# Part of the softmax exps moved from ScalarE to VectorE in a two-layer transformer kernel

## The chip, the cores and the metric

The kernel runs on one core of one Trainium2 chip. The metric is the time of one execution on the device in microseconds (us), lower is better. An execution is called slow when it is over 1.5% above the fastest of the same kernel; only fast ones are compared. A ratio within 2% of 1 counts as "the same".

A word on terms. A **block** is 128 keys by 512 queries of one head. A **slot** is one step of the main loop: three blocks, thus one exp instruction over 1536 columns. A **segment** is four heads with 512 queries against all 2048 keys: 64 blocks, 21.3 slots. A **chunk** is 512 queries of one layer, all 32 heads: eight segments. **Side work** is everything TensorE does beside attention: projections, output, feed-forward, transposes. A piece of it is **evacuated** when VectorE copies its sum out of PSUM. To **emit** an instruction is to put it into an engine's queue while the kernel is being built; the order is fixed then.

## The reference, cut to what matters

Two layers; in each, attention with 32 heads of 16 on 2048 rows of width 512, then a relu feed-forward of width 1792. Inputs are bf16.

```python
scores = jnp.einsum("bhqd,bhkd->bhqk", q, k) * (Dh ** -0.5)
p = _softmax(scores, axis=-1)
o = jnp.einsum("bhqk,bhkd->bhqd", p, v)
...
x = x + _A_ref(_layernorm(x, axis=-1), A_wqkv, A_wo)     # attention
x = x + _B_ref(_layernorm(x, axis=-1), B_w1, B_w2)       # feed-forward
# both twice, with the same weights
```

The softmax takes 2 x 32 x 2048 x 2048 exps. With 128 lanes that is 2.1 million columns, in 4096 blocks of 512.

## The kernel before: the parts that matter

The main loop. Each slot writes scores for three blocks into one of two PSUM tiles of three banks, one exp reads them all, and the value matmuls of the slot before last follow. Side work is given to TensorE in small pieces by a pace, and VectorE's own queue by a budget.

```python
    while blocks:
        ...
        now = [blocks.popleft() for _ in range(min(W, len(blocks)))]      # W = 3
        b = ps_s[no % 2]                                                   # two tiles, three banks each
        times = 1 if level >= 0 else 2 if level > -1 else 3                # repeats, to keep TensorE busy
        for _ in range(times):
            for w, (sg, kb, g) in enumerate(now):
                nc.tensor.matmul(b[:, w, :], kt[...], qbuf[...], start=True, stop=True, ...)
        ex = nc.scalar.activation(out=eb[:, :m, :], in_=b[:, :m, :], func=ACTF.Exp, scale=SCALE)
        run_evac()
        while len(pend) > 1:
            emit_pv()                                                      # value matmuls into ps_o
        spent = run_pe(pace) if todo else 0.0                              # side work, a little a slot
        level = min(level + times + 1 + spent - FLOOR, 0.4)
        run_dve(900)
```

The function that is used when something must be finished before the loop may go on. Its order: first evacuations, then every piece of TensorE work whose inputs have been emitted, and VectorE's queue last.

```python
    def force():
        if evac:
            run_evac()
            return True
        if cur or pick(emitted):
            cur.popleft()[1]()
            return True
        for i, (c, deps, fn) in enumerate(dve_q):
            if emitted(deps):
                dve_q.pop(i)
                fn()
                return True
        return False

    def run_until(key):
        while key not in made:
            assert force(), key
```

All side work shares one PSUM bank, `ps_f`, during the main loop.

The softmax here doesn't subtract the row's maximum and nothing guards it: scores larger than these inputs give would overflow.

## Time and profile before

| | before |
|---|---|
| median of 4 runs | 2046.97 us (2044.28 to 2048.04) |
| span of the profiled run | 2037.9 us |
| busy: ScalarE, TensorE, VectorE | 92%, 83%, 21% |
| score matmuls (4096 are needed) | 7704 |
| ScalarE idle ahead of exps | 55.1 us |
| mean TensorE clock | 0.971 |

The lines are shown and read in the prediction. One more view of the same trace is the table of waits: who waited for whom, then us in total, times, and the longest.

```profile
PE ps_s L621 <- ACT e L628: 218.8, 604, 0.8
...
ACT e L628 <- PE ps_s L621: 54.2, 109, 2.4
```

The two lines together say which engine leads. TensorE waits for ScalarE four times as long as ScalarE for TensorE, and ScalarE's longest wait is 2.4 us.

### The profile page before, as it was taken

To read this page: it belongs to the slowest core of one execution; us is meant where nothing else is said; L and a number is where in the kernel's file an instruction comes from. 1 tells how busy PE (TensorE), PEld (TensorE's weight loads), DVE (VectorE), ACT (ScalarE), POOL (GpSimd) and SP (SyncE) were. 2 spreads that over 40 slices of the span, in tenths; PEclk is the share of its full clock that TensorE was granted. 3 is DMA by queue.
4 is the path that set the end of the run, shared out by engine and by line. 5 is a ranking of instruction groups with operands and counts; after the bars stand their busy time and mean duration, and the time that the engine had idled before them with its cause. 6 is when DMAs were issued, how large, how long until landed. Compare 5 with 4: busy or idle time off the path is not lost.

```text
span 2037.9 us, 30025 instructions
## 1 busy us (share of the span) xinstructions
PE 1690.9 (83%) x13604; PEld 523.4 (26%) x13604; DVE 436.9 (21%) x927; ACT 1871.7 (92%) x1407; POOL 2.4 (0%) x35
## 2 busy tenths in 40 slices
PE   5777778888888888888889877898888888888876
PEld 2222222222222222222222222222222222222222
DVE  5111102212132132212133220211112111121122
ACT  2799999999999999999989999999999999999960
POOL 0000000000000000000000000000000000000000
PEclk8999999999999999999899989989998999989998
DMA  4000000000000000000000010000000000000000
GB/s 155 1 12 12 12 7 12 12 12 6 12 12 11 7 12 12 10 8 12 12 1 1 4 30 9 9 12 12 17 12 12 10 12 19 12 9 10 17 11 11
DMA packets 34131, 29.42 MB, mean 14 GB/s; under 512 B 17492, under 2 KB 25428, under 8 KB 34004
## 3 DMA queue, kind: packets, MB, share of 16 engines
q1 hardware_dynamic: 32420, 25.94, 5.6%
q8 instruction: 106, 1.74, 0.3%
q10 hardware_dynamic: 1584, 1.57, 0.2%
q14 instruction: 21, 0.17, 0.0%
HBM read 7.86 MB, written 2.10 MB: 5 GB/s over the span
## 4 chain that ended last, share of the span: by engine, by line
ACT 71%; PE 17%; DVE 8%; DMA 3%; issue 1%; SPq 0%; DVEq 0%
ACT e L628 71%; PE ps_s L621 6%; PE ps_f L243 5%; PE ps_o L545 4%; DMA r<-u 2%; PE ps_s L243 2%; DVE u L494 1%; DVE ht L400 1%; DVE q L371 1%; PE ps_s L579 1%; DVE stats L260 1%; DMA u<-c 1%; PE ps_f L298 0%; DVE xn L288 0%; ACT xnT L573 0%
## 5 line engine op out<-in xcount | busy, mean ns | idle before, releaser
L628 ACT ACTIVATE e<-ps_s 128x1536 bf16<-128x1536 f32 x1366 | 1847.9, 1581 | 55.1 <-PE ps_s L621 54.2
L621 PE MATMUL ps_s<-q,ktp 32*128 32x512 bf16 x7704 | 812.2, 385 | 221.2 <-ACT e L628 218.8
L545 PE MATMUL ps_o<-e,vaug 128*32 128x512 bf16 x4096 | 568.7, 396 | 45.3 <-DVE u L494 34.6
L621 PEld LDWEIGHTS <-ktp 32*128 32x128 bf16 x7704 | 257.2, 92 | 714.5 <-issue 659.7
L545 PEld LDWEIGHTS <-vaug 128*32 128x32 bf16 x4096 | 138.1, 93 | 490.3 <-issue 490.3
L243 PE MATMUL ps_f<-xn2T,w 128*128 128x512 bf16 x400 | 121.2, 391 | 11.1 <-DVE q L371 5.1
L400 DVE TENSOR_SCALAR ht<-ps_f 128x512 bf16<-128x512 f32 x99 | 68.4, 691 | 281.0 <-PE ps_f L243 281.0
L243 PE MATMUL ps_f<-w,ht 128*128 128x512 bf16 x406 | 120.0, 383 | 1.0
L499 DVE SCALAR_TENSOR_TENSOR ot<-u,mask,r 128x512 bf16<-128x512 f32 (+1 forms) x67 | 48.7, 727 | 276.5 <-DMA r<-u 273.8
L494 DVE COPY u<-ps_o 128x512 f32<-128x512 f32 x58 | 40.1, 691 | 266.5 <-PE ps_o L545 266.5
L243 PE MATMUL ps_f<-xnT,wqkv 128*128 128x512 bf16 x248 | 74.1, 389 | 1.4 <-DVE vaug L363 0.2
L371 DVE TENSOR_SCALAR q<-ps_f,mask 128x512 bf16<-128x512 f32 x68 | 47.9, 746 | 90.2 <-PE ps_f L243 90.2
L243 PE MATMUL ps_f<-wo,ot 128*128 128x512 bf16 x224 | 66.2, 386 | 0.8
L414 DVE TENSOR_TENSOR x<-x,ps_f 128x512 bf16<-128x512 bf16 x29 | 20.0, 688 | 189.2 <-PE ps_f L243 189.2
L386 DVE TENSOR_TENSOR x<-x,ps_f 128x512 bf16<-128x512 bf16 x28 | 19.2, 687 | 161.1 <-PE ps_f L243 161.1
L243 PEld LDWEIGHTS <-w 128*128 128x128 bf16 x448 | 32.0, 99 | 76.4 <-issue 67.5
L260 DVE BATCH_NORM_STATS2 stats<-x 128x6 f32<-128x512 bf16 x64 | 44.0, 687 | 7.0 <-DMA x<-in_A_x_dram 5.6
L338 DVE CAST ktp<-ps_f 128x512 bf16<-128x512 f32 x28 | 19.4, 692 | 117.1 <-PE ps_f L243 117.1
L243 PEld LDWEIGHTS <-ht 128*128 128x128 bf16 x448 | 29.1, 97 | 57.5 <-issue 47.9
L398 ACT ACTIVATE ht<-ps_s 128x512 bf16<-128x512 f32 x6 | 3.6, 597 | 42.8 <-PE ps_s L243 42.8
L298 PE MATMUL ps_f<-ident,xn 128*128 128x128 bf16 x188 | 21.8, 249 | 16.3 <-DVE xn L288 10.0
L298 PEld LDWEIGHTS <-xn 128*128 128x128 bf16 x256 | 18.4, 109 | 54.6 <-DVE xn L288 31.7
(54 smaller groups left out, 303.1 us busy)
## 6 DMA issues: line engine op xcount, KB each, us to landing
r<-u SPq DMA_DIRECT2D x63, 256.0 KB
w<-in_B_w_dram SPq DMA_DIRECT2D x2, 1792.0 KB
x<-in_A_x_dram SPq DMA_DIRECT2D x16, 128.0 KB
out_dram<-x SPq DMA_DIRECT2D x16, 128.0 KB
wqkv<-in_A_wqkv_dram ACTq DMA_DIRECT2D x3, 512.0 KB
c<-u SPq DMA_DIRECT2D x63, 8.0 KB
u<-c SPq DMA_DIRECT2D x63, 8.0 KB
wo<-in_A_wo_dram SPq DMA_DIRECT2D x1, 512.0 KB
```

Of the source, the lines that this page charges most:

```text
L243: nc.tensor.matmul(b, lhsT, rhs, start=(i == 0), stop=(i == n - 1))
L260: nc.vector.bn_stats(out=st[:], in_=x_t[j * TPC + i][:])
L298: nc.tensor.transpose(pt[:, c * P : (c + 1) * P], xnbuf[i][:, c * P : (c + 1) * P], ident[:])
L371: nc.vector.tensor_scalar(out=qbuf[n % 2][e][:], in0=b, scalar1=mask[e][:, 0:1], scalar2=None, op0=ALU.mult,)
L400: nc.vector.tensor_scalar(out=ht[ft][:], in0=b, scalar1=0.0, scalar2=None, op0=ALU.max)
L414: nc.vector.tensor_add(out=x_t[tt][:], in0=x_t[tt][:], in1=b)
L494: nc.vector.tensor_copy(out=u[:], in_=ps_o[:])
L499: nc.vector.scalar_tensor_tensor(out=ot[t][:, a : a + w], in0=u[:, a : a + w], scalar=mask[e][:, 0:1], in1=r[:, a : a + w], op0=ALU.mult, ...
L545: nc.tensor.matmul(ps_o[32 * g : 32 * g + 32, :], vaug[sg["l"]][kb][:, 4 * sg["T"] + g, 2 * e : 2 * e + 32], s["e"][:, w, :], start=(kb == ...
L579: nc.tensor.matmul(b, lhsT, rhs, start=(i == 0), stop=(i == len(mms) - 1))
L621: nc.tensor.matmul(b[:, w, :], kt[32 * g : 32 * g + 32, kc : kc + P], qbuf[sg["n"] % 2][sg["e"]][32 * g : 32 * g + 32, :], start=True, sto ...
L628: ex = nc.scalar.activation(out=eb[:, :m, :], in_=b[:, :m, :], func=ACTF.Exp, scale=SCALE)
```

## The change

Its intent: ScalarE is the bound and VectorE idles, so in six of a segment's 21 slots the third block's exp is made by VectorE. The queries are scaled so that a score is already in units of 2 to the 23rd per octave; adding 126 x 2^23 and converting to an integer gives the bits of a float whose exponent is right and whose mantissa is linear. Two bit operations and a polynomial in the mantissa give the rest. Of the two parts of the result one is doubled, and the addition is left to the value matmul: three matmuls a block in place of one. The blocks of two slots (a **pair**) share the five long VectorE operations. Because the VectorE values come out divided by 2 x LEAD, the exps on ScalarE get a bias of -ln(2 x LEAD), from a [128,1] tile. Which pairs are taken, and when their operations are emitted, is decided by a counter `load[0]` of VectorE's backlog. The core of the diff (cuts marked):

```diff
+    PAIRS = ((0, 2), (6, 8), (12, 14))
     FLOOR = 3.4
+    BACKLOG = 5000.0
...
-        while i < len(dve_q) and budget > 0:
+        while i < len(dve_q) and load[0] < limit:
...
+    def flush_pair():
+        run_until(pairs[0]["key"])
+        emit_pair()
+
+    def dve_block(half, sg, kb, g, src):
+        while half == 0 and pairs:
+            flush_pair()
+        nc.vector.tensor_scalar(
+            out=di[:, half, :].bitcast(I32), in0=src, scalar1=EXP_BIAS, scalar2=0.0,
+            op0=ALU.add, op1=ALU.max,
+        )
+        load[0] += 690
...
+            dve_q[0:0] = [
+                (650, [], lambda: bits(dm, 0x007FFFFF, 0x3E800000)),
+                (1220, [], lambda: step(dy, dm, C2, dm)),
+                (1220, [], lambda: step(dy, dy, C1, dm)),
+                (1220, [], lambda: step(de, dy, C0, di)),
+                (650, [], last),
+            ]
+
+    def emit_pair():
+        p = pairs.popleft()
...
+        for rhs in (de, de, None):
+            for half, (kb, g) in halves:
+                pv(p["sg"], kb, g, tops[:, half, 1::2] if rhs is None else rhs[:, half, :])
...
+            if half == 0:
+                taken = load[0] + sum(c for c, _, _ in dve_q) < BACKLOG
...
-        ex = nc.scalar.activation(out=eb[:, :m, :], in_=b[:, :m, :], func=ACTF.Exp, scale=SCALE)
+        ex = nc.scalar.activation(
+            out=eb[:, :m, :], in_=b[:, :m, :], func=ACTF.Exp, bias=ebias[:, 0:1],
+            scale=1.0 / (LOG2E * UNIT),
+        )
...
+        load[0] = max(load[0] - 50.0 - 427.0 * m, 0.0)
         run_evac()
+        if half is not None:
+            dve_block(half, sg, kb, g, b[:, W - 1, :])
...
+        if pairs and ready([pairs[0]["key"]]):
+            emit_pair()
...
-        run_dve(900)
+        run_dve(500.0)
```

It also adds, where a segment is finished, `run_until(("m", n - 2))`: the multiply that normalises the segment before last must have been emitted.

More of the change, by code (lines that the diff above doesn't have):

```diff
@@ L1 @@
+import math
 from contextlib import ExitStack
@@ L55 @@
     NACC = 6
+    LEAD, C2, C1, C0 = 0.43216083424908747, -0.036015386827967774, 0.769178243088122, 0.36146642138144963
+    KAPPA_BITS = 0x00170000
+    LOG2E = 1.4426950408889634
+    UNIT = float(1 << 23)
+    EXP_BIAS = 126.0 * UNIT
+    PAIRS = ((0, 2), (6, 8), (12, 14))
     FLOOR = 3.4
+    BACKLOG = 5000.0
     ctx.enter_context(tc.manual_schedule())
@@ L66 @@
     mask = [sb([P, 1], FP32, f"mask{e}") for e in range(2)]
+    qmask = [sb([P, 1], FP32, f"qmask{e}") for e in range(2)]
+    ebias = sb([P, 1], FP32, "ebias")
     wqkv = sb([P, NDC, 3 * D], BF16, "wqkv")
@@ L89 @@
     ot = [sb([P, QS], BF16, f"ot{t}") for t in range(NT)]
-    acc = [sb([P, QS], FP32, f"acc{t}") for t in range(NACC)]
+    dm = sb([P, 2, QS], FP32, "dm")
+    dy = sb([P, 2, QS], FP32, "dy")
+    di = sb([P, 2, QS], FP32, "di")
+    de = sb([P, 2, QS], BF16, "de")
+    acc = [x[:, k, :] for x in (dm, dy, di) for k in range(2)]
     ebuf = [sb([P, W, QS], BF16, f"e{n}") for n in range(NE)]
@@ L121 @@
     nc.gpsimd.memset(warm[:], 0.0)
+    nc.gpsimd.memset(ebias[:], -math.log(2.0 * LEAD))
     nc.scalar.activation(out=warm[:], in_=warm[:], func=ACTF.Exp)
@@ L189, in run_pe, with run_dve @@
         return spent
-    def run_dve(budget):
+    load = [0.0]
+    def run_dve(limit):
         i = 0
-        while i < len(dve_q) and budget > 0:
+        while i < len(dve_q) and load[0] < limit:
             c, deps, fn = dve_q[i]
@@ L197, in run_dve @@
                 fn()
-                budget -= c
+                load[0] += c
             else:
@@ L203, in run_evac @@
         while evac:
-            evac.popleft()()
+            c, fn = evac.popleft()
+            fn()
+            load[0] += c
     def force():
@@ L228, in run_all, with mm_group @@
         assert not (urgent or work or dve_q or cur)
-    def mm_group(mms, fin, deps, per=2):
+    def mm_group(mms, fin, deps, per=2, cost=690):
         hold = {}
@@ L244, in piece @@
                 if a + per >= n:
-                    evac.append(lambda: fin(b))
+                    evac.append((cost, lambda: fin(b)))
             pieces.append((min(per, n - a), piece))
@@ L324, in fin @@
                     mark(("xnT", tag, i))
-                evac.append(fin)
+                evac.append((430, fin))
             groups.append({"pieces": [(1.3, piece)], "deps": [("xn", tag, i)] + war})
@@ L371, in fin @@
                 nc.vector.tensor_scalar(
-                    out=qbuf[n % 2][e][:], in0=b, scalar1=mask[e][:, 0:1], scalar2=None,
+                    out=qbuf[n % 2][e][:], in0=b, scalar1=qmask[e][:, 0:1], scalar2=None,
                     op0=ALU.mult,
@@ L378, in q_group @@
             [(wqkv[:, c, T * P : (T + 1) * P], xnT[j][:, c, :]) for c in range(NDC)],
-            fin, all4("xnT", ("ln1", l, j)),
+            fin, all4("xnT", ("ln1", l, j)), cost=1400,
         )
@@ L460, in add_run @@
                     "l": l, "j": j, "t": 2 * T + e, "e": e, "T": T, "kbs": kbs, "n": n,
-                    "load": load, "store": store,
+                    "load": load, "store": store, "begun": set(),
                 }
@@ L483, in finish_segment @@
         l, j, t, e = sg["l"], sg["j"], sg["t"], sg["e"]
+        load[0] += 690
         if sg["store"]:
-            nc.vector.tensor_copy(out=acc[t][:], in_=ps_o[:])
+            nc.vector.tensor_copy(out=acc[t], in_=ps_o[:])
             return
@@ L488, in finish_segment @@
         norm_no[0] += 1
+        if n > 1:
+            run_until(("m", n - 2))
         u, r, c = ubuf[n % 2], rbuf[n % 2], cbuf[n % 2]
@@ L491, in finish_segment @@
         if sg["load"]:
-            nc.vector.tensor_add(out=u[:], in0=acc[t][:], in1=ps_o[:])
+            nc.vector.tensor_add(out=u[:], in0=acc[t], in1=ps_o[:])
         else:
@@ L504, in mul @@
                 mark(("ot", l, j, t, i))
+            mark(("m", n))
         if last:
@@ L533, with pv @@
     pend = deque()
-    last_exp = [None] * NE
+    exps = [deque(maxlen=6) for _ in range(NE)]
+    def pv(sg, kb, g, rhs, stop=False):
+        e = sg["e"]
+        nc.tensor.matmul(
+            ps_o[32 * g : 32 * g + 32, :],
+            vaug[sg["l"]][kb][:, 4 * sg["T"] + g, 2 * e : 2 * e + 32],
+            rhs, start=g not in sg["begun"], stop=stop,
+            tile_position=(0, 32 * g), skip_group_check=True,
+        )
+        sg["begun"].add(g)
     def emit_pv():
@@ L543, in emit_pv @@
             sg, kb, g, w = s["blocks"].popleft()
-            e = sg["e"]
-            nc.tensor.matmul(
-                ps_o[32 * g : 32 * g + 32, :],
-                vaug[sg["l"]][kb][:, 4 * sg["T"] + g, 2 * e : 2 * e + 32],
-                s["e"][:, w, :],
-                start=(kb == sg["kbs"][0]), stop=(kb == sg["kbs"][-1]),
-                tile_position=(0, 32 * g), skip_group_check=True,
-            )
-            if kb == sg["kbs"][-1] and g == 3:
+            last = kb == sg["kbs"][-1]
+            if last:
+                while pairs and pairs[0]["sg"] is sg:
+                    flush_pair()
+            pv(sg, kb, g, s["e"][:, w, :], last)
+            if last and g == 3:
                 finish_segment(sg, sg is segs[-1])
@@ L555, in emit_pv, with bits, step, last @@
             pend.popleft()
+    pairs = deque()
+    pair_no = [0]
+    def flush_pair():
[3 more added lines that the diff above has]
+        while half == 0 and pairs:
+            flush_pair()
+        nc.vector.tensor_scalar(
+            out=di[:, half, :].bitcast(I32), in0=src, scalar1=EXP_BIAS, scalar2=0.0,
+            op0=ALU.add, op1=ALU.max,
+        )
+        load[0] += 690
+        if half == 0:
+            pair_no[0] += 1
+            pairs.append({"sg": sg, "key": ("e", pair_no[0]), "blocks": []})
+        pairs[-1]["blocks"].append((kb, g))
+        if half == 1:
+            key = pairs[-1]["key"]
+            def bits(out, keep, put):
+                nc.vector.tensor_scalar(
+                    out=out[:].bitcast(I32), in0=di[:].bitcast(I32), scalar1=keep,
+                    scalar2=put, op0=ALU.bitwise_and, op1=ALU.bitwise_or,
+                )
+            def step(out, x, c, y):
+                nc.vector.scalar_tensor_tensor(
+                    out=out[:], in0=x[:], scalar=c, in1=y[:], op0=ALU.add, op1=ALU.mult
+                )
+            def last():
+                bits(di, 0x7F800000, KAPPA_BITS)
+                mark(key)
+            dve_q[0:0] = [
[7 more added lines that the diff above has]
+        p = pairs.popleft()
+        halves = list(enumerate(p["blocks"]))
+        tops = di[:].bitcast(BF16)
+        for rhs in (de, de, None):
+            for half, (kb, g) in halves:
+                pv(p["sg"], kb, g, tops[:, half, 1::2] if rhs is None else rhs[:, half, :])
     for j in range(NQS):
@@ L568 @@
                     op=ALU.add, axis=mybir.AxisListType.XY,
+                )
+            for e in range(2):
+                nc.vector.tensor_scalar(
+                    out=qmask[e][:], in0=mask[e][:], scalar1=SCALE * LOG2E * UNIT, scalar2=None,
+                    op0=ALU.mult,
                 )
@@ L599 @@
     level = 0.0
+    taken = False
     while blocks:
@@ L626 @@
                 )
-        m = len(now)
-        ex = nc.scalar.activation(out=eb[:, :m, :], in_=b[:, :m, :], func=ACTF.Exp, scale=SCALE)
-        if last_exp[no % NE] is not None:
+        sg, kb, g = now[-1]
+        r = (kb * 4 + g - 2) // W
+        half = None
+        if len(now) == W and now[0][0] is sg and not (sg["load"] or sg["store"]):
+            half = next((p.index(r) for p in PAIRS if r in p), None)
+            if half == 0:
+                taken = load[0] + sum(c for c, _, _ in dve_q) < BACKLOG
+            if not taken:
+                half = None
+        m = len(now) - (half is not None)
+        ex = nc.scalar.activation(
+            out=eb[:, :m, :], in_=b[:, :m, :], func=ACTF.Exp, bias=ebias[:, 0:1],
+            scale=1.0 / (LOG2E * UNIT),
+        )
+        for earlier in exps[no % NE]:
             tc.declare_no_dep(
-                ex.ins, last_exp[no % NE],
+                ex.ins, earlier,
                 reason="the matmuls that read the buffer between the two writes order them",
             )
-        last_exp[no % NE] = ex.ins
+        exps[no % NE].append(ex.ins)
+        load[0] = max(load[0] - 50.0 - 427.0 * m, 0.0)
         run_evac()
+        if half is not None:
+            dve_block(half, sg, kb, g, b[:, W - 1, :])
         for sg, kb, g in now:
@@ L639 @@
             emit_pv()
-        pend.append({"e": eb, "blocks": deque(x + (w,) for w, x in enumerate(now))})
+        if pairs and ready([pairs[0]["key"]]):
+            emit_pair()
+        pend.append({"e": eb, "blocks": deque(x + (w,) for w, x in enumerate(now[:m]))})
         rest = len(blocks) / W % per_chunk
@@ L644 @@
         spent = run_pe(pace) if todo else 0.0
+        sg = now[-1][0]
         level = min(level + times + 1 + spent - FLOOR, 0.4)
-        run_dve(900)
+        run_dve(500.0)
     while pend:
```

## The prediction

> **What bounds the kernel now.** I read, in this order, the busy shares, the costliest groups, the chain in order of time, the timeline of a stretch in mid-run, and the busy time of one tile by windows. Busy shares and groups of the page:
>
> ```profile
> PE 1690.9 (83%) x13604; PEld 523.4 (26%) x13604; DVE 436.9 (21%) x927; ACT 1871.7 (92%) x1407; POOL 2.4 (0%) x35
> ...
> L628 ACT ACTIVATE e<-ps_s 128x1536 bf16<-128x1536 f32 x1366 | 1847.9, 1581 | 55.1 <-PE ps_s L621 54.2
> L621 PE MATMUL ps_s<-q,ktp 32*128 32x512 bf16 x7704 | 812.2, 385 | 221.2 <-ACT e L628 218.8
> ...
> L545 PE MATMUL ps_o<-e,vaug 128*32 128x512 bf16 x4096 | 568.7, 396 | 45.3 <-DVE u L494 34.6
> ...
> L400 DVE TENSOR_SCALAR ht<-ps_f 128x512 bf16<-128x512 f32 x99 | 68.4, 691 | 281.0 <-PE ps_f L243 281.0
> ...
> L499 DVE SCALAR_TENSOR_TENSOR ot<-u,mask,r 128x512 bf16<-128x512 f32 (+1 forms) x67 | 48.7, 727 | 276.5 <-DMA r<-u 273.8
> ```
>
> ScalarE makes 1366 exps, each over three 512-column score blocks (a "slot"), and is idle ahead of them for only 55 us. They overlap, so the 1581 ns is not the pace: the chain in order of time has runs such as
>
> ```profile
> 128.49 55.19 ACT e L628 x41
> ```
>
> that is 55.19/41 = 1.346 us a slot. 1366 x 1.346 = 1839 us of the 2038 us span: **ScalarE is the bound** from about 60 us to 1995 us, and VectorE (21%) has room. TensorE looks 83% busy, but 7704 score matmuls run where 4096 blocks need 4096: the rest are repeats that fill a floor of work (FLOOR). How close it runs, from the timeline:
>
> ```profile
> 1002.98 0.39 PE L621 MATMUL ps_s<-q,ktp 32*128 32x512 bf16 x3
> 1003.30 0.10 PEld L545 LDWEIGHTS <-vaug 128*32 128x32 bf16 x3 [0.23 <-issue]
> 1003.30 0.40 PE L545 MATMUL ps_o<-e,vaug 128*32 128x512 bf16 x3
> 1003.63 0.11 PEld L243 LDWEIGHTS <-wqkv 128*128 128x128 bf16 x2 [0.23 <-issue]
> 1003.63 0.60 PE L243 MATMUL ps_f<-xnT,wqkv 128*128 128x512 bf16 x2
> 1004.17 0.19 PEld L621 LDWEIGHTS <-ktp 32*128 32x128 bf16 x3 [0.42 <-issue]
> 1004.26 0.39 PE L621 MATMUL ps_s<-q,ktp 32*128 32x512 bf16 x3
> ```
>
> A slot of TensorE is scores (0.32), values (0.33), two matmuls of projections or feed-forward work (0.54): 1.19 us of 1.346. That side work (1280 matmuls of 512 columns) is spread thinly. The windows of tile ht, the feed-forward hidden, show its shape:
>
> ```profile
> 360.00:390.00 30.00, 0.00 (x0) 0.00 (x0) 4.84 (x7) 0.00 (x0) 1.00 0.05 11
> 390.00:420.00 30.00, 0.00 (x0) 0.00 (x0) 4.14 (x6) 0.00 (x0) 1.00 0.05 10
> 420.00:450.00 30.00, 7.25 (x24) 1.44 (x24) 0.69 (x1) 0.00 (x0) 1.00 0.05 10
> 450.00:480.00 30.00, 9.07 (x30) 1.70 (x30) 0.00 (x0) 0.00 (x0) 1.00 0.06 11
> ```
>
> The columns are window, length, then busy us and count of PE, weight loads, VectorE, ScalarE. 14 hidden groups, then 56 output matmuls, over about 120 us, and ScalarE never notices. This spreading is what I expect the change to break.
>
> **What the Trainium skill says.** "ScalarE: Activation LUTs", section "What ACT_TABLE_LOAD costs": one element per cycle and lane, 0.833 ns an element, back-to-back activations overlap. The trace agrees: 1536 x 0.833 = 1280, plus 66 makes the 1346 ns. "VectorE: DVE Perf Modes", section "The perf-mode tier table": fp32 single-source ops reach 2x from SBUF, 1x from PSUM, two-source fp32 ops 1x. The trace shows 691 ns for 512 columns out of PSUM (agrees with 1x) and has no large fp32 SBUF single-source op. "PSUM — Partial Sum Buffer", section "Engine vs sequencer instructions": the queues of ScalarE and VectorE are strict FIFO, and matmuls start and complete in program order. The trace agrees: at segment ends the value matmul waits for the copy of ps_o (34.6 us in all) and the scores behind it wait along.
>
> **The change part by part.** A segment (one head group, 64 blocks) is 21.3 slots. In six of them (numbers 0,2 / 6,8 / 12,14) the third block goes to VectorE.
>
> *Removed.* 58 segments are whole (32 in layer 0, 26 in layer 1; the 12 store/load ones are excluded): 58 x 6 = 348 blocks, 174 pairs at most. Each takes 512 x 0.833 = 427 ns from ScalarE: at most **149 us**.
>
> *Added on VectorE, per pair.* Two PSUM reads, 2 x 0.69; two bit operations over 1024 columns, by the skill's 2x about 0.69 each (estimate); three scalar_tensor_tensor over 1024, extrapolated from 352 ns at 128 columns and 751 at 512 in the groups by form (1.04 ns an element) to 1.28 each. Sum 1.38 + 1.38 + 3.85 = 6.6 us. With all 174 pairs, 1150 us on top of 437: 78% of the span. Fits as a mean.
>
> *Added on TensorE, per pair.* Six value matmuls in two column groups in place of two: about 0.1 + 3 x 0.22 = 0.75 us in one slot (estimate from the 0.33 us of a value pass and 0.22 of a further one). 174 x 0.75 = 130 us of TensorE, mostly beside ScalarE; but short slots last 0.92 us against about 1.0 of TensorE, so I charge 20 us of stalls.
>
> *Moved.* The schedule is fixed while the kernel is built, by the counter load[0], so I step it by hand. A three-block slot takes 50 + 3 x 427 = 1331 off the counter, and VectorE work is emitted only while it is below 500. After slot 2 the pair's five operations (650, 1220, 1220, 1220, 650) are at the head of the queue: slot 3 emits 650 and stops, slot 4 emits 1220, slot 5 emits 1220. **At slot 6 two of the five are still not emitted**, and the next pair calls flush_pair, then run_until, then force. And force, which the diff leaves alone, first empties every PE piece whose inputs have been emitted, and only then takes from the VectorE queue. So one late pair pours all the available side work into one slot, ahead of the next scores. Every evacuation (690) in a slot also blocks that slot's emission, so pairs are late above all when side work is running.
>
> Does the test "load + queue < 5000" prevent it? At slot 6 without other work: 1220 + (1220 + 650) + 950 (reciprocal and multiply) = 4040: taken, flushed. With one evacuation in slots 3 or 4: 1220 + 3090 + 950 = 5260: not taken, no flush. In slot 5: 690 + 3090 + 950 = 4730: taken, flushed. After slot 14, seven slots remain to the next segment's slot 0, five emissions are needed, and hidden groups evacuate every 2.7 slots (about 150 matmuls left over 100 slots: 1.5 a slot, 4 a group): more often than not late, and flushed. So I expect a flush to hit within one segment of the hidden groups' start, with some 75% of the hidden and output work left.
>
> *Cost of a burst.* One bank ps_f serves all side work, so in a burst a hidden group takes 4 x 0.215 + 0.2 + 0.69 = 1.8 us, an output group 14 x 0.215 + 0.9 = 3.95 us. All of it: 14 x 1.8 + 4 x 3.95 = 41 us; 75% is **31 us with ScalarE idle**. Six chunks (three of each layer; one more runs in the store/load stretch without pairs, one after the loop): 186 us. The k and v groups of layer 0, 8 x 1.8 = 14.4 us a chunk, 60% of three: 26. The first k groups, 12 x 1.8 x 0.7: 15. The o groups, 10.6 us a chunk, 20% of six: 13. Sum 240 us, an estimate; I take 210, as some of it ends under an exp that is under way.
>
> *Blocks really taken.* By the same walk some 8 of 24 pairs a chunk fail the test (slot 6 after a q evacuation of 1400, LayerNorm queues of 7080). Two thirds of 149: **100 us** gained.
>
> *Flushes with nothing to pour.* TensorE stands at the pair's values until VectorE is done. Scores 2 are ready at the start of exp 1 + 0.5; the pair takes 5.9 more; exp 6 starts 6.3 after exp 1. With 0.5 of other VectorE work TensorE goes on at about exp 6 + 0.6, and scores 7 are 1.2 later, when ScalarE wanted them at + 0.9: near 0.8 us each, some 35 times: 30 us.
>
> Sum: 2048 - 100 + 210 + 30 + 20 = 2208. I set **2190 us**, a little lower for the chance that bursts come later in the work than I stepped.
>
> **Rivals.** (1) *The offload works as meant*: pairs are emitted in time, side work stays spread. For it: VectorE is at 21%, ScalarE at 92%, all means fit. Against: the counter leaves two of five operations at slot 6. It would make 2048 - 100..140 + 20..50, near 1970. (2) *TensorE becomes the bound*: 1.0 us plus repeats a slot and 0.75 a pair; the repeats are not reduced for the pairs. For it: 1.19 of 1.346 in the timeline. It would eat half of the gain: 1990 to 2010. (3) *VectorE becomes the bound or holds the score banks*: a block's PSUM read behind 1.28 us operations keeps its bank, and scores two slots on wait. Against: at the first block of a pair the chain is forced out; the mean is 78%. Worth 20 to 60 us. (4) *Bursts of side work*, my choice.
>
> **Range and chances.** With few bursts the time is near 1970, with all of the side work in bursts near 2300. The range is 1975 to 2310. I give slower 0.65, as the walk through the counters leaves little way round it; faster 0.23, for a mis-stepped schedule; same 0.12, where half the bursts meet the gain.
>
> **What would show it.** ScalarE should have about 230 exps of 1024 columns at 0.92 us pace; its idle time should rise from 55 to some 300 us, released by score matmuls, in a few waits of 10 to 40 us. The windows of tile ht should show 14 hidden groups and 56 output matmuls within 30 to 60 us instead of 120, with ScalarE's busy share low there. VectorE should gain 700 to 1000 us, with 1.28 us for the three-step operations and 0.69 for the bit ones. If the longest waits of ScalarE stay under 3 us, the bursts are not there and I am wrong; if the bit operations take 1.2 us, VectorE's sum is too small by 1 us a pair.

## The result, and the profile after

| | before | after |
|---|---|---|
| median of 4 runs | 2046.97 us | 2510.05 us (2504.19 to 2537.47) |
| exps of 1536 and of 1024 columns | 1365, 0 | 1121, 244 |
| ScalarE idle ahead of exps | 55.1 us | 477.4 us |
| score matmuls | 7704 | 8651 |
| busy VectorE | 436.9 us | 1202.4 us |
| mean TensorE clock | 0.971 | 0.901 |

The ratio is 1.2291 (95% interval 1.2201 to 1.2381). A ratio here and below is the mean time of one kernel's fast runs over that of the other's of the same rounds, so not quite the ratio of the medians. The result was correct.

Busy shares and the groups of the changed kernel, in the columns of the prediction's first fence:

```profile
PE 1962.1 (78%) x14923; PEld 595.6 (24%) x15039; DVE 1202.4 (48%) x1783; ACT 1920.7 (77%) x1407; POOL 2.5 (0%) x36
...
L730 ACT ACTIVATE e<-ps_s,ebias 128x1536 bf16<-128x1536 f32 (+1 forms) x1366 | 1896.9, 1478 | 477.4 <-PE ps_s L714 473.1
...
L601 DVE TENSOR_SCALAR di<-ps_s 128x512 int32<-128x512 f32 x244 | 168.8, 692 | 666.0 <-ACT e L730 633.3
...
L620 DVE SCALAR_TENSOR_TENSOR de<-dy,di 128x1024 bf16<-128x1024 f32 x122 | 149.4, 1224 | 3.9
...
L614 DVE TENSOR_SCALAR dm<-di 128x1024 int32<-128x1024 int32 x122 | 84.6, 693 | 3.7
```

Two things stand out. The exps are 244 blocks lighter, 244 x 0.427 = 104 us by the price that the prediction used, and yet their busy time has *risen* from 1847.9 to 1896.9 us. And they wait 422 us longer. The two increases, 49 + 422 = 471 us, are the whole difference of the spans (2509.1 - 2037.9 = 471.2), so all of the loss can be looked for on ScalarE.

**The waits.** From the table of waits:

```profile
DVE di L601 <- ACT e L730: 633.3, 201, 22.5
ACT e L730 <- PE ps_s L714: 473.1, 257, 40.3
...
PE ps_s L714 <- DVE di L601: 69.5, 113, 1.2
```

ScalarE now waits up to 40 us. In the main loop nine waits of 14 to 40 us make up 275 us. One of them, in ScalarE's timeline (start, length, and in brackets the idle time before):

```profile
794.91 5.48 ACT L730 ACTIVATE e<-ps_s,ebias 128x1536 bf16<-128x1536 f32 x4
840.16 2.63 ACT L730 ACTIVATE e<-ps_s,ebias 128x1536 bf16<-128x1536 f32 x2 [39.77 <-PE ps_s L714]
```

What the others did meanwhile, at its start and at its end:

```profile
802.35 1.02 PE L265 MATMUL ps_f<-xn2T,w 128*128 128x512 bf16 x4 [0.78 <-DVE ht L422]
...
803.41 0.69 DVE L422 TENSOR_SCALAR ht<-ps_f 128x512 bf16<-128x512 f32 x1 [1.11 <-PE ps_f L265]
804.16 1.02 PE L265 MATMUL ps_f<-xn2T,w 128*128 128x512 bf16 x4 [0.78 <-DVE ht L422]
...
833.69 0.69 DVE L436 TENSOR_TENSOR x<-x,ps_f 128x512 bf16<-128x512 bf16 x1 [3.27 <-PE ps_f L265]
834.30 1.22 DVE L620 SCALAR_TENSOR_TENSOR dy<-dy,dm 128x1024 f32<-128x1024 f32 x1
835.55 1.23 DVE L620 SCALAR_TENSOR_TENSOR de<-dy,di 128x1024 bf16<-128x1024 f32 x1
836.81 0.69 DVE L614 TENSOR_SCALAR di<-di 128x1024 int32<-128x1024 int32 x1
836.83 1.04 PE L564 MATMUL ps_o<-de,vaug 128*32 128x512 bf16 x4 [3.17 <-DVE de L620]
```

A hidden group starts every 1.81 us (802.35, 804.16): TensorE and VectorE take turns at the one bank. After the last output group come the last three of a pair's five operations, then the pair's values; the next scores and the next exp are behind all that. This is the pouring of side work that the prediction describes. The windows of tile ht, in the prediction's columns, show all 14 hidden groups and all 56 output matmuls within these 60 us, where they were spread over about 120 us before:

```profile
790.00:820.00 30.00, 1.35 (x6) 0.77 (x8) 9.17 (x14) 0.00 (x0) 1.00 0.01 1
820.00:850.00 30.00, 11.27 (x50) 4.67 (x48) 0.00 (x0) 0.00 (x0) 0.76 0.00 1
```

**The pace.** In the stretch without pairs the chain in order of time has

```profile
1397.64 17.30 ACT e L730 x12
```

17.30 / 12 = 1.442 us for an exp of 1536 columns, against 1.346 before. Nothing in the prediction accounts for that. ScalarE is slower by nearly 0.1 us at *every* exp, also where no block goes to VectorE.

**The read.** VectorE waits 633 us in all at its read of the score block, for the *exp*: both read the same PSUM tile, and the second reader has been made to wait for the first. The scores two slots on then wait for VectorE's read (69.5 us).

**The clock.** The trace's clock records know two states, full and half. A score matmul takes 378 ns in the mean in the first and 613 in the second. With a mean of 0.901 the changed kernel stood 2 x (1 - 0.901) x 2509, about 498 us, at the half clock; the kernel before stood there 122 us. Two windows around the wait above, all engines (busy us and count of PE, weight loads, VectorE, ScalarE, GpSimd; then the clock):

```profile
780.00:840.00 60.00, 41.69 (x233) 15.59 (x236) 22.34 (x32) 19.26 (x15) 0.00 (x0) 0.96 0.02 4
840.00:900.00 60.00, 56.13 (x360) 12.75 (x359) 24.39 (x49) 51.52 (x35) 0.00 (x0) 0.61 0.05 10
```

After the burst TensorE runs at a mean of 0.61, is busy 56 of 60 us, and only 35 exps fit in where 41 would at 1.442 us each. So this stall is followed by a stretch in which TensorE is slow as well. What such stretches are worth was not tested by a run of its own. Within the four executions of the changed kernel, which run the same program, the time rises by about 0.25 us for each further us at half clock (2504 us at 0.910, 2537 at 0.885). By that figure the 376 us more at half clock are some 90 us of the loss; this is an estimate, and those us are inside what the experiments below charge to the three causes.

### The profile page after: what moved, and what is told of

Read it like the earlier page. It is cut to its first block, busy times and chain, and to the rows that moved or that the text cites. A ratio compares the mean times of both kernels' runs of the same rounds, so it can differ in the third digit from the quotient of the medians.

```text
span 2509.1 us, 33820 instructions
## 1 busy us (share of the span) xinstructions
PE 1962.1 (78%) x14923; PEld 595.6 (24%) x15039; DVE 1202.4 (48%) x1783; ACT 1920.7 (77%) x1407; POOL 2.5 (0%) x36
## 4 chain that ended last, share of the span: by engine, by line
ACT 48%; PE 33%; DVE 15%; issue 3%; DMA 1%; another core or an unknown queue 0%; SPq 0%; DVEq 0%; ACTq 0%
ACT e L730 47%; PE ps_s L714 13%; PE ps_f L265 9%; PE ps_o L564 8%; DVE di L601 3%; DVE dy L620 2%; DVE ht L422 2%; DVE de L620 1%; PE ps_s L265 1%; DVE u L519 1%; DVE x L436 1%; PE ps_s L671 1%; DVE dm L614 1%; DVE q L393 1%; DVE ktp L360 1%
## 5 line engine op out<-in xcount | busy, mean ns | idle before, releaser
L730 ACT ACTIVATE e<-ps_s,ebias 128x1536 bf16<-128x1536 f32 (+1 forms) x1366 | 1896.9, 1478 | 477.4 <-PE ps_s L714 473.1
L714 PE MATMUL ps_s<-q,ktp 32*128 32x512 bf16 x8651 | 964.6, 417 | 262.7 <-ACT e L730 186.9
L601 DVE TENSOR_SCALAR di<-ps_s 128x512 int32<-128x512 f32 x244 | 168.8, 692 | 666.0 <-ACT e L730 633.3
L620 DVE SCALAR_TENSOR_TENSOR de<-dy,di 128x1024 bf16<-128x1024 f32 x122 | 149.4, 1224 | 3.9
L620 DVE SCALAR_TENSOR_TENSOR dy<-dy,dm 128x1024 f32<-128x1024 f32 x122 | 149.3, 1224 | 3.8
L620 DVE SCALAR_TENSOR_TENSOR dy<-dm 128x1024 f32<-128x1024 f32 x122 | 149.3, 1224 | 3.5
L564 PE MATMUL ps_o<-de,vaug 128*32 128x512 bf16 x488 | 94.3, 440 | 51.0 <-DVE de L620 51.0
L265 PE MATMUL ps_f<-w,ht 128*128 128x512 bf16 x393 | 93.9, 379 | 20.2 <-DVE x L436 14.4
L614 DVE TENSOR_SCALAR di<-di 128x1024 int32<-128x1024 int32 x122 | 84.6, 693 | 3.9
L614 DVE TENSOR_SCALAR dm<-di 128x1024 int32<-128x1024 int32 x122 | 84.6, 693 | 3.7
L564 PE MATMUL ps_o<-di,vaug 128*32 128x512 bf16 x244 | 62.8, 450 | 3.7 <-DVE di L614 1.7
```

The lines of the kernel that those rows point to most:

```text
L265: nc.tensor.matmul(b, lhsT, rhs, start=(i == 0), stop=(i == n - 1))
L564: nc.tensor.matmul(ps_o[32 * g : 32 * g + 32, :], vaug[sg["l"]][kb][:, 4 * sg["T"] + g, 2 * e : 2 * e + 32], rhs, start=g not in sg["begun ...
L601: nc.vector.tensor_scalar(out=di[:, half, :].bitcast(I32), in0=src, scalar1=EXP_BIAS, scalar2=0.0, op0=ALU.add, op1=ALU.max,)
L614: nc.vector.tensor_scalar(out=out[:].bitcast(I32), in0=di[:].bitcast(I32), scalar1=keep, scalar2=put, op0=ALU.bitwise_and, op1=ALU.bitwise_or,
L620: nc.vector.scalar_tensor_tensor(out=out[:], in0=x[:], scalar=c, in1=y[:], op0=ALU.add, op1=ALU.mult)
L714: nc.tensor.matmul(b[:, w, :], kt[32 * g : 32 * g + 32, kc : kc + P], qbuf[sg["n"] % 2][sg["e"]][32 * g : 32 * g + 32, :], start=True, sto ...
```

## The experiments

Each is a small edit. "Changed kernel" is the kernel after the change. Of each the time is the median of four runs; the kernel before had medians of 2043.57 to 2047.43 us beside them. The first four take the three suspected costs one at a time.

### e1: the bias alone, in the kernel before

```diff
-ex = nc.scalar.activation(out=eb[:, :m, :], in_=b[:, :m, :], func=ACTF.Exp, scale=SCALE)
+ex = nc.scalar.activation(out=eb[:, :m, :], in_=b[:, :m, :], func=ACTF.Exp, bias=ebias[:, 0:1], scale=SCALE)
```

(`ebias` is a tile of zeros.)

> The kernel before, with one thing of the change alone: the exp takes its bias from a [128,1] tile (of zeros). Theory 'the pointer bias costs': the exp pace goes from 1.346 to about 1.432 us as in the changed kernel, so the time rises by 1366 x 0.086 = 117 us to about 2164 us. Rival 'the slower pace comes from the pairs': no change, 2047 us.

Measured 2169.79 us, ratio 1.0609 (1.0572 to 1.0646). That is 126 us over the 2043.57 of the kernel before, or 126 / 1366 = 92 ns an exp. The bias tile costs more than the whole offload was to gain (100 us by the prediction). The profiled execution of this kernel was an odd one of 4667.67 us with matmuls of 982 ns; it is left out of the comparison, and no view of its trace serves here.

### e2: only the pair's own operations are flushed

```diff
 def flush_pair():
-    run_until(pairs[0]["key"])
+    while pairs[0]["key"] not in made:
+        dve_q.pop(0)[2]()
     emit_pair()
```

> The changed kernel, but a late pair is finished by taking only its own VectorE operations from the head of the queue, so no side work is poured out with it. Theory 'bursts': the nine waits of 14 to 40 us (275 us together) go, hidden groups are spread again, time about 2240 us. Rival 'the side work only finds another place to stall, the pairs themselves cost': at most 60 us gained, above 2440 us.

Measured 2276.62 us, ratio 1.1128: 233 us less than the changed kernel, with 234 blocks on VectorE in place of 244. ScalarE's waits for scores fell from 473 to 237 us:

```profile
ACT e L731 <- PE ps_s L715: 237.1, 235, 24.9
```

Three waits of 11 to 25 us were left, 49 us together, and they are in e6 and e8 too. The trace of e6 shows what they are: the output groups are poured, then VectorE makes a reciprocal and stands 8.6 us at the DMA that brings it to the normalising multiply. That is the other `run_until`, which the change added at a segment's end; the pairs ahead in the queue had starved the two operations until it forced them.

### e3: no bias tile

The factor moves into the constant of the VectorE values, so the result stays correct.

```diff
-EXP_BIAS = 126.0 * UNIT
+EXP_BIAS = (126.0 + math.log2(2.0 * LEAD)) * UNIT
...
-func=ACTF.Exp, bias=ebias[:, 0:1],
+func=ACTF.Exp,
```

> The changed kernel, but the factor 2 x LEAD is folded into the exponent constant of the VectorE values, so that the exp needs no bias tile. Theory 'the pointer bias costs': about 117 us less, 2390 us. Rival: no change, 2510 us.

Measured 2414.46 us, ratio 1.1802: 96 us less. The pace is back; the chain in order of time has

```profile
1339.65 13.55 ACT e L728 x10
```

13.55 / 10 = 1.355 us. It gains 96 us here and not the 126 of e1. The likely reason, not tested, is that in this kernel ScalarE stands still for 494 us, where a shorter exp gains nothing.

### e4: VectorE's read does not wait for the exp

```diff
+tc.declare_no_dep(
+    rd.ins, ex_now[0],
+    reason="both only read the score banks, and different banks of them",
+)
```

> The changed kernel, but VectorE's read of its score block no longer waits for the exp of the same slot (both only read, in different banks). Theory 'this wait delays the scores of two slots on by 0.7 us and stalls ScalarE': 244 blocks x 0.2 to 0.4 us, 50 to 100 us less, about 2430 us, and the waits of VectorE on the exp (633 us) turn into waits on the score matmuls. Rival 'hidden': within 20 us of 2510 us.

Measured 2393.08 us, ratio 1.1667: 117 us less, more than expected. The result stayed correct, and the waits moved as the theory says:

```profile
ACT e L735 <- PE ps_s L719: 381.9, 169, 40.7
DVE di L602 <- PE ps_s L719: 362.1, 153, 19.0
...
DVE di L602 <- ACT e L735: 59.3, 18, 24.0
```

VectorE now waits for the scores themselves. ScalarE's waits went from 257 to 169; the 40 us ones are all still there, so it is the short ones that went.

### e5: the emission limit raised from 500 to 1300

```diff
-run_dve(500.0)
+run_dve(1300.0)
```

> The changed kernel with one number changed: VectorE work is emitted while the counter is below 1300 instead of 500, so that a pair's five operations are emitted by slot 5 when no evacuation comes between. The flush code stays as it is. Theory 'pairs are late because the counter emits one operation a slot': most of the bursts go without any change of the flush, at least 120 us less, 2300 to 2390 us, though more blocks are taken (293 in place of 244). Rival 'the counter has no part, the segment ends force the flush anyway': within 50 us of 2510 us.

Measured 2763.67 us, ratio 1.3536: 254 us *more*. I had expected the pairs to be ready in time. Stepping the counter again, with the 690 of a finished segment in it, leaves the fifth operation unemitted at slot 6: one late operation is enough for a flush. The limit also let more pairs through (312 blocks were taken), so there were more flushes; waits of 3 us and more were 35 with 417 us, against 15 with 296 in the changed kernel. The run says that nearly in time is as bad as late; it does not say that the counter is the cause. That needed e9 and e13.

### e6, e7, e8: the three cures together, and two refinements

e6 has e2, e3 and e4 in one. e7 adds the limit of 1300. e8 adds to e6 that a pair's value matmuls count as TensorE work when the repeats are decided.

> The changed kernel with the three cures together: only the pair's own operations are flushed, no bias tile, VectorE's read not behind the exp. If the three causes are separate and add up: 2510 - 233 - 96 - 117 = about 2064 us. If two of them share waits: 2090 to 2150 us. If the offload is sound once its three costs are gone: below 2044 us.

> The three cures together and the emission limit of 1300: 325 blocks on VectorE, 325 x 0.427 = 139 us off ScalarE. If ScalarE is the bound again, about 40 us below the kernel with the three cures. If TensorE (repeats plus three value matmuls a block) or VectorE now holds the slots, no better than it.

> The three cures, and the pair's six value matmuls counted in the level that decides the repeats of the score matmuls (fewer repeats, some 7125 score matmuls). Theory 'TensorE is near its limit in pair slots': 20 to 40 us below the kernel with the three cures alone. Rival 'repeats only fill idle time': the same within 10 us, or slower if the clock falls.

e6 measured 2075.69 us, ratio 1.0155 (1.0113 to 1.0198). The three single gains add up to 446 us; together they gave 434. So their gains hardly overlap, and together they account for 434 of the 463 us between the medians, with whatever the half clock adds to each (e6 stood there 143 us in place of 498). e7 measured 2160.56 us: more blocks, and no gain from them. TensorE stood 69 us at `de` of the pairs, and ScalarE's waits of 1 to 3 us rose to 109 with 178 us. e8 measured 2069.10 us, 7 us below e6, short of the 20 to 40 that the theory gave and within the 10 of its rival, that repeats fill idle time.

By the 2% rule e6 and e8 count as the same as the kernel before. What keeps e6 above it? Its exp group:

```profile
L734 ACT ACTIVATE e<-ps_s 128x1536 bf16<-128x1536 f32 (+1 forms) x1366 | 1766.2, 1407 | 176.3 <-PE ps_s L718 171.8
```

Busy time fell by 82 us (1847.9 to 1766.2), waits rose by 121 us (55.1 to 176.3), net +39.5 for a span that grew by 35.9. Of the waits, 49 us are the three forced ones of e2; the rest are short.

### e9 and e13: does lateness trigger the pouring?

e9 emits the five operations at once behind the second block, past the counter; the flush code is the original one, but no pair can be late any more.

```diff
-dve_q[0:0] = [ (650, [], ...), ..., (650, [], last) ]
+for _, _, fn in [ (650, [], ...), ..., (650, [], last) ]:
+    fn()
+load[0] += 4960
```

> The changed kernel, but a pair's five operations are emitted at once behind its second block, past the counter, so that no pair can be late; the flush code stays as it is. The run with the limit of 1300 was a poor test, as there the fifth operation was still left at slot 6. Theory 'late pairs pour the side work': the waits of 14 to 40 us go as they did when only the pair's own operations were flushed, time 2230 to 2300 us with 260 blocks. Rival 'the pouring has another trigger': above 2450 us.

It measured 3269.53 us, ratio 1.5979, with 306 blocks where 260 were expected. The time is a clear miss. But no wait of ScalarE is over 14.4 us, so the pouring is gone. In its place there is this, at every pair:

```profile
PE ps_o L564 <- DVE de L620: 716.1, 153, 5.3
```

The values of a pair were now emitted one slot after its operations, TensorE takes its queue in order, and it stood about 5 us at each pair with the next scores behind it. These 716 us are not all of ScalarE's 1224 us of waits for scores: the mean clock fell to 0.735 besides, 1737 us at half clock. e13 therefore emits the operations at once and the values five slots later (`mark(key, 4)`), or four where the next pair begins.

> The changed kernel, a pair's five operations emitted at once behind its second block, its value matmuls at the earliest five slots later; the flush code stays as it is. Theory 'late pairs pour the side work': no wait of ScalarE over 15 us is left, and the 6 us stalls of the eager run go too: 2230 to 2330 us. Rival 'the pouring has another trigger': waits of 30 to 40 us remain, above 2450 us.

It measured 2665.55 us, ratio 1.3028: above the 2450 us at which the rival was to stand. Yet the sign of the rival, waits of 30 to 40 us, is absent: the longest is 14.4 us, and in e5, where pairs were late by one operation, it was 42.1. So lateness does trigger the pouring. The time has a part that neither theory had:

```profile
PE ps_f L265 <- DVE ht L422: 126.5, 30, 6.6
```

Five operations in a row are 5 us of VectorE. An evacuation behind them comes 5 us late, TensorE stands at the next piece of side work, which wants the bank, and the scores stand behind it. All of TensorE's waits for evacuations of `ps_f` come to 273 us in e13, against 36 in e2, the other run without pouring by late pairs. These 237 us more stand beside 389 us more of time. How much of the one is in the other is not shown, as e13 also took 306 blocks against 234 and stood 849 us at half clock against 344. The counter that makes pairs late is also what keeps evacuations prompt.

### e10: pouring alone, in the kernel before

No block goes to VectorE; at slots 6 and 12 of each whole segment all side work that can be emitted is.

```diff
 run_evac()
+sg, kb, g = now[-1]
+if (kb * 4 + g - 2) // W in (6, 12) and now[0][0] is sg and not (sg["load"] or sg["store"]):
+    while evac or cur or pick(emitted):
+        if evac:
+            run_evac()
+        else:
+            cur.popleft()[1]()
```

> The kernel before with the pouring alone: at slots 6 and 12 of every whole segment all side work whose inputs are emitted is issued at once; no block goes to VectorE. Theory: hidden and output groups take 41 us a chunk with ScalarE idle, with the other groups 250 to 350 us over the run, so 2300 to 2400 us. Rival 'pouring is harmless without the load of the pairs': below 2150 us.

Measured 2402.96 us, ratio 1.1752 (1.1733 to 1.1772): 357 us from pouring and nothing else, just above what was expected. The profiled execution was the one slow run of four (2459.46 us), so its sizes are not used, only their kind:

```profile
406.34 6.82 ACT L628 ACTIVATE e<-ps_s 128x1536 bf16<-128x1536 f32 x5 [35.78 <-PE ps_s L621]
```

A wait as long as those of the changed kernel, with VectorE at 18%. The pouring needs no load on VectorE.

### e11 and e12: two runs with a fault

They were to put the normalising operations ahead of the pairs, e12 also with pairs spaced by seven slots.

> The three cures, the pairs counted in the level of the repeats, and the two operations that normalise a segment put ahead of the pairs in VectorE's queue (in the kernel with the three cures they were starved until a forced wait of 10 to 25 us, three in the run, 49 us together). Theory: 2069 - 49 = about 2020 us, below the kernel before. Rival 'the pairs stall ScalarE as much as they save': 2044 us or more.

> The same with the pairs spaced by seven slots (0 and 2, 7 and 9, 14 and 16), so that the counter has time to emit all five operations: 277 blocks in place of 215. If ScalarE is the bound: 62 x 0.427 = 26 us below the run with spacing six. If every pair costs TensorE a wait for VectorE that ScalarE feels: no better, or worse.

e11 measured 2237.41 us with a **wrong** result (relative error 0.079), e12 2447.08 us with a correct one. The fault was mine: the flush of e2 takes whatever is at the head of the queue, and with this edit that could be a normalising multiply whose reciprocal had not been emitted. Nothing follows from either time.

### e14 to e18: the rest of the loss

e14 repeats e11 with separate queues, e15 adds pairs seven slots apart (0 and 2, 7 and 9, 14 and 16), e16 the pair's values one slot later. All have the cures of e8. The core of it:

```diff
-        i = 0
-        while i < len(dve_q) and load[0] < limit:
-            c, deps, fn = dve_q[i]
+        for q in (norm_q, pair_q, dve_q):
+            i = 0
+            while i < len(q) and load[0] < limit:
+                c, deps, fn = q[i]
```

> The three cures, the pairs counted in the level of the repeats, and separate queues for the normalising operations (first when ready), the pairs (second) and the rest. Theory 'the rest of the loss is the starved normalisation, 49 us in three waits, plus a few late pairs': 2010 to 2030 us, 1 to 1.5% below the kernel before. Rival 'each pair costs ScalarE what it saves': 2045 us or more.

> As the run before, with the pairs spaced by seven slots, so that fewer have to be flushed. If flushes are what is left: 10 to 30 us below it. If they are hidden: the same within 10 us.

> As the run before, with the value matmuls of a pair one slot later, so that TensorE does not stand at them while VectorE ends the pair. If TensorE's waits for the pair (16 us in the run with the accounting) reach ScalarE: 10 to 20 us below it. If they are hidden: the same within 10 us.

They measured 2096.16, 2109.21 and 2111.63 us (ratios 1.0253, which is unclear by the 2% rule, 1.0311 and 1.0310): three misses. The three long waits went, as meant; short ones took their place. In e14 VectorE stood 131 us at the DMA that brings the reciprocals, now that the multiply was emitted as soon as the counter of slots allowed. Wider spacing and later values, as they were tried, gained nothing.

e17 lets the multiply come eight slots after its DMA is issued instead of four, and no longer books flushed operations in the counter. e18 takes only two pairs a segment, ten slots apart.

```diff
-mark(("r", n), 4)
+mark(("r", n), 8)
...
-    PAIRS = ((0, 2), (6, 8), (12, 14))        # e18 only
+    PAIRS = ((1, 3), (11, 13))
```

> As e14 (three cures, repeats counted, separate queues), with the normalising multiply allowed eight slots after its DMA instead of four, so that VectorE does not stand at the DMA (131 us in e14). If that stand is what reaches ScalarE: about 60 us below e14, 2030 to 2045 us. If pairs cost TensorE and the evacuations as much as they save: 2070 us or more.

> As e17 with two pairs a segment, ten slots apart (1 and 3, 11 and 13), so that none has to be flushed: fewer blocks (218 in place of 258, 17 us more for ScalarE). If crowding on VectorE is what is left: below e17, 2020 to 2040 us. If not: some 17 us above e17.

e17 measured 2066.86 us, ratio 1.0076: 29 us below e14, half of what was hoped. e18 measured **2028.90 us** (2013.70 to 2041.93), ratio 0.9908 (0.9848 to 0.9968). It is the one version below both kernels, by 0.9%, with a correct result. The interval excludes 1, but by the 2% rule this too is "the same". The profiled execution is the fastest of the four, 2013.70 us. The four follow the clock: 2013.70 us at 0.969, 2021.36 at 0.963, 2036.45 at 0.952, 2041.93 at 0.946. Its exp group and waits:

```profile
L747 ACT ACTIVATE e<-ps_s 128x1536 bf16<-128x1536 f32 (+1 forms) x1366 | 1767.6, 1421 | 109.2 <-PE ps_s L731 105.5
```

```profile
ACT e L747 <- PE ps_s L731: 105.5, 141, 4.8
...
PE ps_o L573 <- DVE de L636: 2.7, 2, 2.5
```

ScalarE's busy time is that of e6 though only 218 blocks are taken in place of 234, and its waits are 67 us shorter; 49 of these are the three forced waits, gone since e14. TensorE hardly stands at the pairs (2.7 us, against 40.8 in e17 and 69 in e7). With ten slots between pairs the operations are done when the values come, without emitting them in a row. In e17, with three pairs six slots apart and otherwise the same code, the waits were 172.7 us. e17 and e18 ran on one chip, the others on others; the kernel before varied by 0.2% between these chips.

## Why the prediction was right or wrong, point by point

It gave 2190 us, with a range to 2310; the kernel took 2510. The direction and the main mechanism were right. Two costs were missing from the sum, a price on the exp and the wait of VectorE's read, and they are most of the 320 us by which it was too small: its 2208 us (before rounding down to 2190) become 2444 with the 96 us of e3 and the 117 of e4 added and 233 in place of 210 for the pouring. The last 66 us are not traced to single terms.

- **The pouring: right, a little small.** The prediction stepped the counter, found two of five operations missing at slot 6, and saw that the flush empties side work first. It put 1.8 us on a hidden group (1.81 in the trace) and 210 us on all of it. Nine waits of 14 to 40 us make 275 us, and taking the pouring out of the flush gained 233. The initial k groups were the largest error: 15 us against a wait of 35.85 us. All twelve groups were poured in place of 70%, and each took 2.65 us in the trace instead of 1.8, as the mean clock from 60 to 120 us was 0.59.
- **The blocks taken: right.** Two thirds of 174 pairs would be 116; 122 were taken, 104 us of exps against 100.
- **The cost on VectorE: right.** 1.22 us for a step (1.28 foretold), 0.69 for the bit operations, 765 us more busy time (700 to 1000 foretold).
- **The exp itself: a step that failed.** The prediction's list of what is added has ScalarE only under "Removed", and keeps the 1.346 us pace for the exps that stay. The bias operand stands in the diff, and was given no term at all. The prediction had checked the price of an exp with a remainder ("1280, plus 66") and had not asked what the remainder is made of. The operand cost 126 us alone in the kernel before (e1), and 96 us in this one (e3). The page of the skill that was quoted for the exp's price states the price of such an operand a sentence away.
- **The read of the score block: the other step that failed, mis-sized and for the wrong reason.** Rival 3 has VectorE's read hold the bank "behind 1.28 us operations", 20 to 60 us, and it did not enter the sum. The read was held by the exp of its own slot instead, an order that the framework sets between two readers of one tile. Removing it gained 117 us (e4).
- **"Flushes with nothing to pour", 30 us, and the 20 us of TensorE stalls: not measured apart.** They are in what remains of e6, where the waits without the three forced ones are about 127 us against 55 before: 72 us for the two terms' 50. The forced waits themselves, 49 us from the second `run_until`, had no term in the prediction.
- **Rival 1, the offload as meant, "near 1970":** wrong too. With the three costs taken away nearly the same pairs (117 in place of 122) gave 2076, not 1970. The gain of 100 us was real on ScalarE (82 in busy time) and was given back in waits: the 49 us that were forced, and 72 us of short ones. The reading offered for the short ones is that each pair puts an errand of TensorE and of VectorE ahead of what ScalarE needs next; no run isolates it. How this divides between the waits at pairs and those at evacuations was not settled; nor was how much of e18's gain comes from fewer pairs and how much from their distance.
- **The clock: no term.** The prediction did not ask what stalls do to TensorE's clock. The mean fell from 0.971 to 0.901. Some 90 us of the loss is the estimate above, and it lies inside the three causes; no run holds the clock and changes only the stalls.

## What to carry to other kernels

Before offloading from a saturated engine, price *every* edit on its remaining instructions, also those that look like mere constants: one operand at 92 ns, 1366 times, cost 126 us where 100 were to be gained. A "finish this now" in a schedule that is fixed at build time should finish only what is asked, since whatever it drags along stands in front of the bound engine's next input. And work given to an idle engine must fit between that engine's errands for the others in time as well as in the mean: here a queue that was half empty made the scores late whether the work came late (pouring), early (TensorE stands at it) or in a row (evacuations stand behind it), and only fewer, wider-spaced pairs came out ahead, by 0.9%. Before explaining a spread between executions of one kernel, set their times beside their clocks: in e18 they sort in the same order.

## What the Trainium skill lacked or had wrong

- "ScalarE: Activation LUTs", section "What ACT_TABLE_LOAD costs", has the price of a [128,1] operand (about 93 ns) but also says that back-to-back activations overlap by about 93 ns, and not whether the one hides the other. It does not: in a saturated chain of exps the bias tile cost 92 ns each (126 us over 1366).
- "VectorE: DVE Perf Modes", section "The perf-mode tier table", has no row for scalar_tensor_tensor and no column for int32. No page gives a time for either. Over 1024 columns in SBUF scalar_tensor_tensor took 1.224 us with fp32 inputs, which fits the table's 1x for two sources; tensor_scalar with two int32 bit operations took 0.693 us, which fits its 2x for fp32.
- "TensorE: Matmul & The Clock Gate", section "Seeing it yourself", warns that clock records are unreliable and that the clock was seen stuck at a quarter for over 50 us. One execution of e1 ran its score matmuls at 982 ns in the mean, against 385 before, over the whole 4666 us. Its trace holds no clock record at all, so that its mean clock reads 1.000. Whether it is the same thing is open; the other three runs of that kernel were within 0.1%.
